# Parts of v side by side in one tile, with the sums over parts moved from PSUM accumulation to DVE and POOL

## The chip, the cores and the metric

The kernel runs on one core of one Trainium2 chip. The metric is the device time of one execution in microseconds (us). A core has a matrix engine (PE, with its weight loads shown apart as PEld), a vector engine (DVE), a scalar engine (ACT), a general engine (POOL) and a queue engine for transfers (SP); they run side by side, each through its own list of instructions in order, and wait for each other by semaphores. PE writes only to PSUM, eight banks of 512 four-byte words in each of 128 partitions; POOL doesn't touch PSUM here.

## What is computed

A recurrent attention (mLSTM) over 4 batches, 8 heads, 768 steps and a head size of 40, and behind it a bilinear feed-forward layer over the 3072 x 320 result. All is float32.

```python
for t in range(S):
    m_new = np.maximum(f_gate[:, :, t] + m, i_gate[:, :, t])
    f_stab = np.exp(f_gate[:, :, t] + m - m_new)
    i_stab = np.exp(i_gate[:, :, t] - m_new)
    C = f_stab * C + i_stab * outer(v_t, k_t)
    n = f_stab * n + i_stab * k_t
    y[:, :, t] = sigmoid(o_t) * (C @ q_t) / max(|n . q_t|, 1)
...
x = y.transpose(0, 2, 1, 3).reshape(3072, 320)
out = ((x @ w_a) * (x @ w_b)) @ w_out          # d_ff = 1536
```

## The kernel before

**Attention in chunks.** The sequence is cut into 6 pieces of 128 steps; with 4 batches that makes 24 chunks (n = 0 to 23, c the piece, b the batch). Within a chunk the recurrence is written as a masked product: a 128 x 128 matrix of weighted scores per head, E, times v, plus what the state from earlier pieces contributes. `va` holds v with two columns added (a one, for the sum n . q, and a zero), so DV = 42 columns a head.

**Precision.** Chunks 0 to 5 (`begin_*`) use float32 products. From chunk 6 on (`stage_*`) a float32 value is written as three bf16 parts, and a product as the six partial products that matter. `top(x)` is the upper half of each float32 word, read in place as bf16. `stage_v(n)` makes v's parts on POOL: v itself (its upper half is part 0), `vr` = v less part 0 (its upper half is part 1), and `vl` = vr less part 1, stored as bf16. `stage_b(n, hf)` makes those of the scores P for four heads each (hf = 0, 1): `pb[:, 0]`, `mid` (in the gbc tile) and `pb[:, 1]`.

**Stages of a chunk**, in the order of the program: B (scores, and `stage_i`, the part of the state, which sets `num`), D (`stage_d` of the chunk before: transposes into xh and xl, the input of the dense layer), E and A (exponentials, and parts of q, k and v, of the next chunk), C (`stage_c`: scores times v, line 603, and DVE's addition to `num`, line 610), U (`stage_u`: the new state, and its parts cb, sent through DRAM to cx), F (`stage_f`: `den`, then POOL's product with the gate, then DVE's with `num`, lines 669 to 686).

**The dense layer.** Chunks are grouped into blocks of 2 or 3 (`sizes`); `moe_block(kb)` runs 12 slices of the hidden layer over a block: the up products (line 810), evictions on ACT and DVE (lines 816 to 821), the down products (line 781). While block kb runs, the attention of the next block is interleaved with it: the code generator yields after each piece, and a scheduler then lays out each engine's list by program order and readiness. PE's list is thus dense products with attention products put between.

**Buffers around the change.** PSUM tiles of attention (pS, pI, pX, pV, pU) come from the pool `ps_at`, two banks in turn; a new one waits until the one two before has been read. `tmp` (two SBUF buffers) holds temporaries. Chunk n uses `va[n % 2]`. `gates_m` is a tile used only at the start, for the gate sums. `weigh(n)`, called from `stage_c`, puts POOL's product vw (line 585) ahead of the state products.

Of the kernel before, what the change touches and what calls it, by code (L numbers as in the profile page):

```python
# [8 lines left out]
F32 = mybir.dt.float32  # L9
BF16 = mybir.dt.bfloat16  # L10
# [5 lines left out]
ALU = mybir.AluOpType  # L16
# [4 lines left out]
def kernel(  # L21
# [13 lines left out]
    nc = tc.nc  # L35
    B, H, S, D = q.shape
    DM, DFF = w_a.shape
    P = 128
    NC = S // P
    NF = DFF // P  # L40
    BH = B * H
    DV = D + 2
# [10 lines left out]
    wpool = ctx.enter_context(tc.tile_pool(name="wpool", bufs=1))  # L53

    rpool = ctx.enter_context(tc.tile_pool(name="rpool", bufs=1))
    apool = ctx.enter_context(tc.tile_pool(name="apool", bufs=2))
# [3 lines left out]
    ps_at = ctx.enter_context(tc.tile_pool(name="ps_at", bufs=2, space=PSUM))  # L60
# [7 lines left out]
    NQ = 2  # L68

    qk = [[wpool.tile([P, H, 64], F32, name=f"{x}{j}") for x in "qk"] for j in range(NQ)]  # L70
    va = [wpool.tile([P, H, DV], F32, name=f"va{j}") for j in range(NQ)]
    for x in qk:
        for y in x:
            nc.gpsimd.memset(y[..., D:], 0.0)
# [6 lines left out]
    HH = H // 2  # L81
# [22 lines left out]
    x = ident[0:BH, 0:BH].rearrange("k (x j) -> k x j", j=2)  # L104
# [74 lines left out]
    def nat(n):  # L179
        return inner.get(n) or (qk[n % NQ], va[n % NQ])  # L180
# [46 lines left out]
    def top(x):  # L227

        return x.bitcast(BF16).rearrange("p h (d w) -> p h d w", w=2)[:, :, :, 1]

    REST = (NC - 1) * P
    gates_m = wpool.tile([3 * BH, REST], F32, name="gates_m")

    def gates_load():
        f, i = (apool.tile([P, S], F32, tag="pb", name=f"g_{x}")[0:BH] for x in "fi")
# [289 lines left out]

    def stage_v(n):
        s = st[n]
        x = nat(n)[1]
        vr = apool.tile([P, H, DV], F32, tag="vr", name=f"vr{n}")
        vl = apool.tile([P, H, DV], BF16, tag="vl", name=f"vl{n}")  # L530
        s["vb"] = (top(x), top(vr), vl)
        nc.gpsimd.tensor_tensor(vr, x, top(x), op=ALU.subtract)
        yield
        nc.gpsimd.tensor_tensor(vl, vr, top(vr), op=ALU.subtract)
        yield
# [46 lines left out]
    def weigh(n):  # L582
        c, b = chunks[n]
        vw = apool.tile([P, H, DV], F32, tag="vw", name=f"vw{n}", bufs=1)
        nc.gpsimd.tensor_tensor(  # L585
            vw, nat(n)[1], w_col(c, b).unsqueeze(2).broadcast_to([P, H, DV]), op=ALU.mult
        )
        vws[n] = vw

    def stage_c(n):  # L590
        c, b = chunks[n]
        s = st[n]
        vb = s["vb"]
        num = s.get("num")
        if c < NC - 1:
            weigh(n)
        pV = ps_at.tile([P, 512], F32, tag="pat", name=f"pV{n}")
        pv = pV[:, 0:H * DV].rearrange("p (h d) -> p h d", h=H)
        terms = ((0, 0), (0, 1), (0, 2), (1, 0), (1, 1), (2, 0))
        for h in range(H):  # L600
            pb = s[f"pb{h // HH}"]
            for x, (i, j) in enumerate(terms):
                nc.tensor.matmul(  # L603
                    pv[:, h], pb[i][:, h % HH, :], vb[j][:, h],
                    start=(x == 0), stop=(x == len(terms) - 1),
                )
            if h % 8 == 8 - 1:
                yield
        if c > 0:
            nc.vector.tensor_tensor(num, pv, num, op=ALU.add)  # L610
        else:
            s["num"] = pv
        yield

    def stage_u(n):
# [104 lines left out]
    def attention():  # L720
        for n in range(NS, NCH):
# [4 lines left out]
            for o in "BDEACUF":  # L726
# [8 lines left out]
                elif o == "B":  # L735
                    yield from stage_b(n, 0)
                    yield from stage_b(n, 1)
                    yield from stage_i(n)
                elif o == "D":
                    if n > NS:  # L740
                        yield from stage_d(n - 1)
                    if n % B == 0 and n > 0:
                        load_o(n // B)
                elif o == "E":
                    if n + 1 < NE:
                        yield from begin_e(n + 1)
                    elif n + 1 < NCH:
                        yield from stage_e(n + 1)
                elif o == "A":
                    if n + 1 < NCH:  # L750
                        yield from stage_a(n + 1)
                        yield from stage_v(n + 1)
                elif o == "U":
                    if NE <= n + 2 < NCH:
                        load_g(n + 2)
                    u = stage_u(n)
                    yield next(u, None)
                    late.append(u)
                    if len(late) > 2:
                        yield from late.pop(0)  # L760
                else:
                    yield from {"C": stage_c, "F": stage_f}[o](n)
# [295 lines left out]
    def rest():  # L1058
        if NS < NE:
            yield from begin_e(NS)  # L1060
        if NS < NF32:
            yield from begin_a(NS)
        else:
            yield from stage_a(NS)
            yield from stage_v(NS)
        if NS >= NE:
            yield from stage_e(NS)
        yield from attention()
# [49 lines left out]
```

## Time and profile before

| | us |
|---|---|
| three runs | 565.04, 560.58, 564.60 |
| median | 564.6 |
| the profiled execution | 560.51 |
| its span, first to last instruction | 558.5 |
| mean granted PE clock in it | 0.993 of full |

A row of the profile names a line of the kernel, an engine and an operation, what it writes and reads (out<-in, numbers of buffers left out), the shape, and a count. In the rows by group, "| 9.1, 503 | 5.5 <-PE" is the busy time in us, the mean of one in ns, and how long the engine sat idle ahead of them and for whom. In the timeline, the first two numbers are the start and the length in us. The length of a PE product is that of its passage through the array; the next one starts long before it ends.

### The profile page before, as it was taken

To read this page: it belongs to the slowest core of one execution; us is meant where nothing else is said; L and a number is where in the kernel's file an instruction comes from. 1 tells how busy PE (TensorE), PEld (TensorE's weight loads), DVE (VectorE), ACT (ScalarE), POOL (GpSimd) and SP (SyncE) were. 2 spreads that over 40 slices of the span, in tenths; PEclk is the share of its full clock that TensorE was granted. 3 is DMA by queue.
4 is the path that set the end of the run, shared out by engine and by line. 5 is a ranking of instruction groups with operands and counts; after the bars stand their busy time and mean duration, and the time that the engine had idled before them with its cause. 6 is when DMAs were issued, how large, how long until landed. Compare 5 with 4: busy or idle time off the path is not lost.

```text
span 558.5 us, 12726 instructions
## 1 busy us (share of the span) xinstructions
PE 544.9 (98%) x4925; PEld 518.0 (93%) x4925; DVE 389.4 (70%) x888; ACT 267.9 (48%) x645; POOL 126.9 (23%) x188
## 2 busy tenths in 40 slices
PE   8999999899999999999999999999999999999997
PEld 6898898799999899999989999998999999999997
DVE  6889999964858683968749774977757755944332
ACT  5574678752626761556525654644526733310111
POOL 3102414641232320332031330333021302000000
PEclk9799999999999999999999999999999999999999
DMA  9999941393649762569536684586539704200001
GB/s 191 215 263 291 290 72 51 94 179 71 108 103 193 141 139 58 123 142 180 107 99 156 108 151 115 118 145 138 118 97 154 144 0 115 48 1 25 0 1 35
DMA packets 198551, 66.75 MB, mean 120 GB/s; under 512 B 184220, under 2 KB 191772, under 8 KB 198492
## 3 DMA queue, kind: packets, MB, share of 16 engines
q1 hardware_dynamic: 198444, 65.86, 56.4%
q8 instruction: 38, 0.62, 0.5%
q14 instruction: 21, 0.17, 0.1%
q10 hardware_dynamic: 48, 0.10, 0.0%
HBM read 41.11 MB, written 5.95 MB: 84 GB/s over the span
## 4 chain that ended last, share of the span: by engine, by line
PE 60%; DMA 17%; DVE 10%; ACT 5%; issue 3%; SPq 3%; POOL 1%; ACTq 0%; DVEq 0%; POOLq 0%
PE pu L810 31%; PE pd L781 15%; DMA T<-qks 4%; DMA c_dram<-cb 3%; ACT gbc L490 3%; DMA va<-in_v_dram 2%; PE pV L603 2%; PE pU L628 2%; DVE gbc L554 2%; DMA gbc<-g_dram 1%; DMA raw<-in_moe_w_a_dram 1%; DVE pb L556 1%; PE pS L884 1%; PE pV L927 1%; PE pS L545 1%
## 5 line engine op out<-in xcount | busy, mean ns | idle before, releaser
L810 PE MATMUL pu<-xh,w 128*128 128x384 f32 (+1 forms) x1080 | 276.5, 324 | 2.6 <-ACT g L816 0.9
L810 PE MATMUL pu<-xl,w 128*128 128x384 f32 (+1 forms) x648 | 208.0, 322 | 0.0
L810 PEld LDWEIGHTS pu<-xh,w 128*128 128x128 f32 x1080 | 190.6, 189 | 5.9 <-ACT g L816 1.3
L781 PE MATMUL pd<-w,gh 128*128 128x320 f32 x576 | 126.7, 309 | 0.0
L810 PEld LDWEIGHTS pu<-xl,w 128*128 128x128 f32 x648 | 122.2, 189 | 0.2
L817 DVE TENSOR_TENSOR g<-pu,g 128x384 f32<-128x384 f32 (+1 forms) x108 | 54.6, 505 | 89.4 <-PE pu L810 46.3
L781 PEld LDWEIGHTS pd<-w,gh 128*128 128x128 f32 x576 | 96.7, 188 | 0.1
L781 PE MATMUL pd<-w,gl 128*128 128x320 f32 x288 | 85.3, 310 | 0.0
L816 ACT COPY g<-pu 128x384 f32<-128x384 f32 (+1 forms) x90 | 39.6, 440 | 93.4 <-PE pu L810 84.2
L490 ACT ACTIVATE gbc<-gbc,gtab 128x128 f32<-128x128 f32 x160 | 49.1, 389 | 18.1 <-POOL gbc L483 18.0
L821 DVE TENSOR_TENSOR gl<-g,gh 128x384 fp32r<-128x384 f32 (+1 forms) x92 | 52.2, 568 | 1.9
L781 PEld LDWEIGHTS pd<-w,gl 128*128 128x128 f32 x288 | 53.1, 188 | 0.2
L585 POOL TENSOR_TENSOR vw<-va,gtab 128x336 f32<-128x336 f32 x20 | 16.4, 822 | 160.3 <-PE pU L628 135.2
L819 DVE CAST gh<-g 128x384 fp32r<-128x384 f32 (+1 forms) x108 | 41.1, 382 | 2.2
L483 POOL TENSOR_SCALAR_AFFINE_SELECT gbc<-gbc 128x1024 f32<-128x1024 f32 x20 | 22.6, 1132 | 65.1 <-DMA gbc<-g_dram 32.9
L554 DVE TENSOR_TENSOR gbc<-gbc,pb 128x512 f32<-128x512 f32 x36 | 27.2, 757 | 6.8 <-ACT pb L552 6.6
L603 PEld LDWEIGHTS <-pb 128*128 128x128 bf16 x576 | 23.4, 96 | 6.4 <-DVE pb L556 3.2
L684 POOL TENSOR_TENSOR osig<-osig,den 128x320 f32<-128x320 f32 x22 | 16.6, 754 | 54.9 <-DVE den L671 42.9
L603 PE MATMUL pV<-va,pb 128*128 128x42 bf16 x288 | 25.9, 183 | 2.7 <-DVE pb L556 2.7
L790 ACT COPY o<-pd 128x320 f32<-128x320 f32 x24 | 8.8, 434 | 40.3 <-PE pd L781 40.3
L550 DVE TENSOR_TENSOR gbc<-pS,gbc 128x512 f32<-128x512 f32 x36 | 23.7, 682 | 4.0 <-PE pS L545 4.0
L518 ACT COPY qks<-qks 128x640 bf16<-128x640 bf16 x36 | 26.0, 725 | 0.6
(154 smaller groups left out, 849.6 us busy)
## 6 DMA issues: line engine op xcount, KB each, us to landing
gbc<-g_dram SPq DMA_DIRECT2D x20, 512.0 KB
q<-in_q_dram SPq DMA_DIRECT2D x24, 160.0 KB
k<-in_k_dram SPq DMA_DIRECT2D x24, 160.0 KB
va<-in_v_dram SPq DMA_DIRECT2D x24, 160.0 KB
osig<-in_o_gate_dram SPq DMA_DIRECT2D x24, 160.0 KB
raw<-in_moe_w_out_dram SPq DMA_DIRECT2D x12, 320.0 KB
out_dram<-o SPq DMA_DIRECT2D x24, 160.0 KB
raw<-in_moe_w_a_dram SPq DMA_DIRECT2D x8, 384.0 KB
```

The lines of the kernel that those rows point to most:

```text
L483: nc.gpsimd.affine_select(E, E, pattern=[[0, H], [1, P]], compare_op=ALU.is_ge, fill=-1e30, base=0, channel_multiplier=-1,)
L490: nc.scalar.activation(E[:, h], E[:, h], AF.Exp, bias=beta[:, h:h + 1])
L518: nc.scalar.copy(qks[:, 0, :, lo:lo + 2 * D], qks[:, 1, :, D - lo:3 * D - lo])
L550: nc.vector.tensor_tensor(E, pS, E, op=ALU.mult)
L554: nc.vector.tensor_tensor(E, E, pb[:, 0], op=ALU.subtract)
L603: nc.tensor.matmul(pv[:, h], pb[i][:, h % HH, :], vb[j][:, h], start=(x == 0), stop=(x == len(terms) - 1),)
L781: nc.tensor.matmul(pd[t][:, 0:DM], a[:, cols], w, start=(ff == 0 and first), stop=(ff == NF - 1 and last),)
L810: nc.tensor.matmul(acc[j], a, r, start=(x == 0), stop=(x == len(terms) - 1),)
L816: (nc.vector.tensor_copy if ff in [1, 2] else nc.scalar.copy)(g, acc[0])
L817: nc.vector.tensor_tensor(g, acc[1], g, op=ALU.mult)
L819: nc.vector.tensor_copy(gh, g)
L821: (nc.gpsimd if kb * 12 + ff < 16 else nc.vector).tensor_tensor(gl, g, gh.bitcast(F32), op=ALU.subtract)
```

## The change

The three parts of v move into one float32 tile `v3[j]` of shape [128, 3, 8, 42], part by part; `va[j]` is its first third. `vr` and `vl` are the other thirds, and `vl` is now stored as float32 and read by its upper half like the others. `gates_m` takes the place of the later thirds of `v3[1]`, which are not in use yet at that time.

In `stage_c` the products of a head are no longer one for each pair of parts. Part i of P meets the parts 0 to 2 - i of v in one product, of 126, 84 or 42 columns. What belongs to each part of v stays in its own group of 42 columns, and one half of the heads (4 x 3 x 42 = 504 words) fills one PSUM bank. DVE then adds the three groups of a head out of the bank (a `tensor_reduce` that reads the groups as the innermost axis) into a `tmp` tile, and POOL adds that to `num`. A chunk has two halves, so two banks of `ps_at`, two reductions and two POOL additions, and one yield more than before.

```diff
-    va = [wpool.tile([P, H, DV], F32, name=f"va{j}") for j in range(NQ)]
+    v3 = [wpool.tile([P, 3, H, DV], F32, name=f"va{j}") for j in range(NQ)]
+    va = [x[:, 0] for x in v3]
...
-    gates_m = wpool.tile([3 * BH, REST], F32, name="gates_m")
+
+    gates_m = v3[1].rearrange("p w h d -> p (w h d)")[0:3 * BH, H * DV:H * DV + REST]
...
-        x = nat(n)[1]
-        vr = apool.tile([P, H, DV], F32, tag="vr", name=f"vr{n}")
-        vl = apool.tile([P, H, DV], BF16, tag="vl", name=f"vl{n}")
-        s["vb"] = (top(x), top(vr), vl)
+        x, vr, vl = (v3[n % NQ][:, i] for i in range(3))
...
-        pV = ps_at.tile([P, 512], F32, tag="pat", name=f"pV{n}")
-        pv = pV[:, 0:H * DV].rearrange("p (h d) -> p h d", h=H)
-        terms = ((0, 0), (0, 1), (0, 2), (1, 0), (1, 1), (2, 0))
-        for h in range(H):
-            pb = s[f"pb{h // HH}"]
-            for x, (i, j) in enumerate(terms):
-                nc.tensor.matmul(
-                    pv[:, h], pb[i][:, h % HH, :], vb[j][:, h],
-                    start=(x == 0), stop=(x == len(terms) - 1),
-                )
-            if h % 8 == 8 - 1:
-                yield
-        if c > 0:
-            nc.vector.tensor_tensor(num, pv, num, op=ALU.add)
-        else:
-            s["num"] = pv
+
+        vb = v3[n % NQ].bitcast(BF16).rearrange("p i h (d w) -> p h i d w", w=2)[..., 1]
+        for hf in range(2):
+            pV = ps_at.tile([P, 512], F32, tag="pat", name=f"pV{n}_{hf}")
+            pv = pV[:, 0:HH * 3 * DV].rearrange("p (h i d) -> p h i d", h=HH, i=3)
+            pb = s[f"pb{hf}"]
+            for x in range(HH):
+                for i in range(3):
+                    nc.tensor.matmul(
+                        pv[:, x, 0:3 - i], pb[i][:, x, :], vb[:, hf * HH + x, 0:3 - i],
+                        start=(i == 0), stop=(i == 2),
+                    )
+            yield
+            t = apool.tile([P, H * DV], F32, tag="tmp", name=f"v{n}_{hf}")[:, 0:HH * DV]
+            t = t.rearrange("p (h d) -> p h d", h=HH)
+            nc.vector.tensor_reduce(
+                t, pv.rearrange("p h i d -> p h d i"), axis=mybir.AxisListType.X, op=ALU.add
+            )
+            y = num[:, hf * HH:(hf + 1) * HH]
+            nc.gpsimd.tensor_tensor(y, t, y, op=ALU.add)
```

The scheduler lays out all engines' lists anew behind the first `stage_c`. First place: DVE at the end of the last chunk (23), from the last half's products to `den` and the product with the gate. Names are tiles; line 610 is the addition before and the reduction after, lines 817 to 821 (now 819 to 823) are evictions of the dense block, 669 to 671 (671 to 673) make den, 685 (687) is the product with num. Before:

```order
L610 TENSOR_TENSOR num_7269<-pV_7298,num_7269 128x336
L669 TENSOR_SCALAR den_7354<-num_7269 128x8
L670 TENSOR_TENSOR den_7354<-num_7269,den_7354 128x8
L671 RECIPROCAL den_7354<-den_7354 128x8
L817 TENSOR_TENSOR g_7_7464<-pu_7_1_7455,g_7_7464 128x256
L819 CAST gh_7_7475<-g_7_7464 128x256
L821 TENSOR_TENSOR gl_7_7477<-g_7_7464,gh_7_7475 128x256
L685 TENSOR_TENSOR osig_6358<-num_7269,osig_6358 128x320
```

Between the reduction and den two instructions of the dense block now stand, while POOL adds to num, and one eviction stands ahead of the product with num. After:

```order
L819 TENSOR_TENSOR g_9_7165<-pu_9_1_7156,g_9_7165 128x256
L610 TENSOR_REDUCE v_1_6991<-pV_1_6977 128x168
L821 CAST gh_9_7176<-g_9_7165 128x256
L823 TENSOR_TENSOR gl_9_7178<-g_9_7165,gh_9_7176 128x256
L671 TENSOR_SCALAR den_6997<-num_6929 128x8
L672 TENSOR_TENSOR den_6997<-num_6929,den_6997 128x8
L673 RECIPROCAL den_6997<-den_6997 128x8
L819 TENSOR_TENSOR g_10_7196<-pu_10_1_7187,g_10_7196 128x256
L687 TENSOR_TENSOR osig_6076<-num_6929,osig_6076 128x320
```

The chunk's end has moved from slice 7 of the dense block to slices 9 and 10 (the first number behind g). Second place: PE where the last block (8) begins. pX is the transpose of chunk 23, pd and pu are the dense block's down and up products, and a pu of 128x384 belongs to block 8. Before, at pX:

```order
L810 MATMUL pu_9_0_7516<-xh_6347,w_1332 128x256
L707 MATMUL pX_7363<-ident,osig_6358 128x128 x2
L810 MATMUL pu_9_0_7516<-xh_6347,w_1352 128x256
L810 MATMUL pu_9_0_7516<-xl_6348,w_1352 128x256
L810 MATMUL pu_9_1_7517<-xh_6347,w_1306 128x256
L707 MATMUL pX_7363<-ident,osig_6358 128x128
```

It stood in slice 9, with 66 products of block 7 left behind it ahead of block 8's first one. After:

```order
L783 MATMUL pd_1_6573<-w_1374,gh_9_7176 128x320 x2
L709 MATMUL pX_7008<-ident,osig_6076 128x128 x3
L783 MATMUL pd_1_6573<-w_1374,gl_9_7178 128x320
L783 MATMUL pd_0_6572<-w_1403,gh_10_7207 128x320 x2
L783 MATMUL pd_0_6572<-w_1403,gl_10_7209 128x320
L783 MATMUL pd_1_6573<-w_1403,gh_10_7207 128x320 x2
L783 MATMUL pd_1_6573<-w_1403,gl_10_7209 128x320
L783 MATMUL pd_0_6572<-w_1417,gh_11_7238 128x320 x2
L783 MATMUL pd_1_6573<-w_1417,gh_11_7238 128x320 x2
L812 MATMUL pu_0_0_7269<-xh_6769,w_311 128x384
L812 MATMUL pu_0_1_7270<-xh_6769,w_367 128x384
```

All of block 7's up products now stand ahead of pX, 11 down products are left between it and block 8, and block 8 begins with products that need xh alone.

More of the change, by code (lines that the diff above doesn't have):

```diff
@@ L592, in stage_c @@
         s = st[n]
-        vb = s["vb"]
-        num = s.get("num")
+        num = s["num"]
         if c < NC - 1:
             weigh(n)
-        pV = ps_at.tile([P, 512], F32, tag="pat", name=f"pV{n}")
-        pv = pV[:, 0:H * DV].rearrange("p (h d) -> p h d", h=H)
-        terms = ((0, 0), (0, 1), (0, 2), (1, 0), (1, 1), (2, 0))
-        for h in range(H):
-            pb = s[f"pb{h // HH}"]
-            for x, (i, j) in enumerate(terms):
-                nc.tensor.matmul(
-                    pv[:, h], pb[i][:, h % HH, :], vb[j][:, h],
-                    start=(x == 0), stop=(x == len(terms) - 1),
-                )
-            if h % 8 == 8 - 1:
-                yield
-        if c > 0:
-            nc.vector.tensor_tensor(num, pv, num, op=ALU.add)
-        else:
-            s["num"] = pv
+        vb = v3[n % NQ].bitcast(BF16).rearrange("p i h (d w) -> p h i d w", w=2)[..., 1]
[17 more added lines that the diff above has]
+            nc.gpsimd.tensor_tensor(y, t, y, op=ALU.add)
         yield
```

## The prediction

> **What bounds the kernel.** I read the page's busy times first, then the stretches, the rows of the line that changes, and the waits.
>
> ```profile
> PE 544.9 (98%) x4925; PEld 518.0 (93%) x4925; DVE 389.4 (70%) x888; ACT 267.9 (48%) x645; POOL 126.9 (23%) x188
> PE 60%; DMA 17%; DVE 10%; ACT 5%; issue 3%; SPq 3%; POOL 1%; ACTq 0%; DVEq 0%; POOLq 0%
> 300.00:370.00 70.00, 69.67 (x706) 67.05 (x705) 51.41 (x116) 36.84 (x87) 17.73 (x23) 1.00 0.69 136
> 440.00:500.00 60.00, 60.00 (x590) 59.41 (x589) 38.86 (x92) 18.89 (x48) 5.25 (x6) 1.00 0.26 55
> ```
>
> The last two rows are stretches: start and end, length, then busy time of PE, PEld, DVE, ACT and POOL, granted clock, DMA. PE is busy from end to end at full clock, in the attention stretches too. So PE's instruction stream is the time, and work on DVE, ACT or POOL counts only where PE comes to wait for it. The span is 558.5 us, the profiled execution took 560.5 us, and the median of the three runs is 564.6 us (the others 560.6 and 565.0); I add up against 560.5 us, the low end of the runs.
>
> How far the PE waits now for other engines, and what the changed product costs there:
>
> ```profile
> PE pV L603 <- DVE pb L556: 2.7, 5, 0.9
> PE pX L707 <- DVE gbc L550: 1.0, 2, 0.7
> DVE osig L685 <- POOL osig L684: 3.5, 5, 0.8
> POOL cb L653 <- DVE cb L652: 17.2, 9, 3.4
> L603 PE MATMUL pV<-va,pb x288: 180/182/195, 119.9 to 489.6; 128*128 128x42 bf16 x144
> L603 PEld LDWEIGHTS <-pb 128*128 128x128 bf16 x576 | 23.4, 96 | 6.4 <-DVE pb L556 3.2
> 488.58 1.22 PE pV L603 x48
> 290.06 1.07 PE L545 MATMUL pS<-T,T 120*128 120x128 bf16 x16
> 295.00 0.57 PE L571 MATMUL pI<-cx,T 120*128 120x42 bf16 x16
> ```
>
> The first four rows are who waited for whom, total us, times, longest. In the fifth a product lasts 182 ns, but that is its way through the array; they overlap. What a product costs is the step to the next one. A weight load lasts 96 ns (sixth row) and overlaps likewise. The seventh row, from the chain of waits, is one whole chunk: 48 products in 1.22 us, 25.4 ns each, 152 ns for a head's six. The eighth gives the step at 128 columns: 16 products in 1.07 us, the last one lasting 0.22 us, so (1.07 - 0.22) / 15 = 57 ns. The ninth, likewise with 0.18 us, gives 26 ns at 42 columns.
>
> **The change on PE.** It concerns 18 chunks (n = 6 to 23), 144 heads. Each head's six products of 42 columns become three of 126, 84 and 42. The columns are the same, 252; what goes is the floor that a narrow product pays. 126 columns: 56 ns, just under the 57 of the row at 128. 42 columns: 25 ns, as now. 84 columns: no row; it lies between 25 and 57 ns, and a straight line between the two rows gives 41. Sum 122 ns against 152: 30 ns a head, 144 x 0.030 = 4.3 us off PE. The bounds: with 84 at 25 ns 46 ns a head, 6.6 us; at 57 ns 14 ns a head, 2.0 us. The weight loads go from 864 to 432; they overlap the products (16 loads and 16 products in that 1.07 us), so they are not counted again.
>
> The Trainium skill (TensorE: Matmul & The Clock Gate, Back-to-back issue gap) speaks against this: it gives about 81 ns a product as the sustained step at 128 columns in a stream of loads and products. By it, 126 would cost 81 and 84, on the line from 25, some 53; a head 159 ns, and the change would add 1.0 us. This trace's stream of such pairs shows 57 ns, so I take the row; the same section's table, 60 cycles up to 64 columns and 134 at 128, fits the rows.
>
> **The change on DVE and POOL.**
>
> ```profile
> L610 DVE TENSOR_TENSOR num<-pV,num 128x336 f32<-128x336 f32 x18 | 9.1, 503 | 5.5 <-PE pV L603 5.5
> L550 DVE TENSOR_TENSOR gbc<-pS,gbc 128x512 f32<-128x512 f32 x36 | 23.7, 682 | 4.0 <-PE pS L545 4.0
> L554 DVE TENSOR_TENSOR gbc<-gbc,pb 128x512 f32<-128x512 f32 x36 | 27.2, 757 | 6.8 <-ACT pb L552 6.6
> L647 POOL TENSOR_TENSOR cr<-cst,cb 128x168 f32<-128x168 f32 x18 | 11.0, 610 | 0.1
> L106 DVE TENSOR_REDUCE sides<-ident x1: 170/170/170, 2.0 to 2.0; 32x2 f32<-32x32 f32 x1
> ```
>
> Removed: one DVE addition a chunk, 18 x 0.503 = 9.1 us. Added: 36 reductions, each reading 4 x 42 x 3 = 504 elements of PSUM. The only reduction in the trace is tiny (0.17 us), so the price comes from the elementwise rows: as it reads 504 elements of PSUM, it is nearest to the 512 of L550, 0.68 us; not under the 336 elements of L610 at 0.50, and I bound it above by L554's 0.76. 36 x 0.68 = 24.5 us, so DVE gains 15.4 us (9 to 18), 389 to 405 us. In the stretch 300 to 370, with four chunks, it goes from 51.4 to about 55 of 70 us: still cover, but less. POOL gets 36 additions of 168 elements, the size of L647, 36 x 0.61 = 22 us, 127 to 149 us, on an engine idle for three quarters. The two subtractions of stage_v stay on POOL; that they write 4-byte words to one tile costs nothing that PE sees. Moving gates_m into v3[1] has no price: everything ahead of the first stage_c stands in the same order on all engines.
>
> The chain within a chunk grows. Here is its end in the last chunk, and the start of the last block that needs it:
>
> ```profile
> 489.84 0.51 DVE L610 TENSOR_TENSOR num<-pV,num 128x336 f32<-128x336 f32 x1 [1.49 <-PE pV L603]
> 490.79 0.20 DVE L671 RECIPROCAL den<-den 128x8 f32<-128x8 f32 x1
> 491.07 0.73 POOL L684 TENSOR_TENSOR osig<-osig,den 128x320 f32<-128x320 f32 x1 [10.44 <-DVE den L671]
> 492.32 0.48 DVE L685 TENSOR_TENSOR osig<-num,osig 128x320 f32<-128x320 f32 x1
> 493.22 0.25 ACT L686 COPY osig<-osig 128x64 f32<-128x64 f32 x1
> 495.31 0.38 PE L707 MATMUL pX<-ident,osig 128*128 128x128 f32 x2
> 496.76 0.56 DVE L712 TENSOR_TENSOR xl<-pX,xh 128x384 fp32r<-128x384 f32 x1 [1.27 <-ACT xh L711]
> 504.20 0.34 PE L810 MATMUL pu<-xh,w 128*128 128x384 f32 x1
> ...
> 489.80 1.27 PE pu L810 x10
> 502.89 1.47 PE pd L781 x10
> ```
>
> (The last two rows, from the chain of waits, give the dense block's steps there: 127 ns at 256 columns, 147 ns in the down products.) In place of L610's 0.51 stand a reduction (0.68), an addition on POOL (0.61) and two hand-overs of about 0.1 (from the reciprocal's end to POOL's start is 0.08): 1.0 us more. POOL runs in order, so an addition can stand behind the cr and cb of stage_u (POOL waited 17.2 us for DVE there), and DVE's den waits behind it with the dense block's evictions queued after it. The last xl ends at 497.3 and block 8 begins at 504.2: 6.9 us of room, against three chunks x 1.0 = 3.0 us. The planned order, though, uses that room up (front, second order): 11 down products, 11 x 0.147 = 1.6 us, stand between pX and block 8's first, where 66 stood. It holds as long as the chain keeps to the plan: from the last pV to pX stand 17 down and 32 up products, 17 x 0.147 + 32 x 0.127 = 6.6 us, against a chain of 0.68 + 0.81 (reduction, POOL addition with hand-overs) + 0.64 (den, from 490.35 to 490.99) + 0.91 (POOL again) + 0.48 + 0.25 (L685, L686) = 3.8 us.
>
> PSUM: a chunk now takes seven ps_at banks in turn instead of six, out of two, and the one that pV_0 held goes to pU only when the reduction has read it. The five waits for pb cost 2.7 / 5 = 0.54 us each. If the 36 reductions are hit as often as those 18 chunks (5 in 18), that is 10 x 0.54 = 5.4 us; if the split, which puts up to 23 dense products between the halves, takes the old waits away too, it is -2.7 us. I take +1.5 us, nearer to the low rows since the order leaves dense work between.
>
> **Sum.** 560.5 - 4.3 + 1.5 = 557.7 us for an execution like the profiled one, 0.5% less. Two of the three runs lie 4 us higher, so I put the time at 558.5 us.
>
> **Rivals.**
> (a) Gain in full and more: the 84 columns come near the floor (6.6 us) and no wait is added: 560.5 - 6.6 = 553.9 us; or the halves also end the pb waits (2.7 us): 551.2 us; the middle is 552.5. For it: five of 18 products wait now and the new order parts the halves. Against it: new waits on banks.
> (b) PE waits for the reductions' banks. The reduction stands in DVE's queue behind an eviction of the dense block that itself waits for PE, as L610 did (5.5 us of waits), and pU, pS and pX wait behind it. Slower by 1% needs 5.6 + 4.3 = 9.9 us, 0.28 us for each of 36. If every second one costs the 0.54 us of a pb wait, that is 9.7 us, and 560.5 - 4.3 + 9.7 = 566 us. For it: only two banks, room at block 8 planned away. Against it: PE's waits on DVE in attention are under 4 us now in 108 hand-overs. The Trainium skill (VectorE: DVE Perf Modes, Rules for kernel authors) calls this reduction the slowest DVE operation and advises against it on a hot path; no long one is in this trace.
> (c) No gain on PE: wide products whose loads are not hidden. It decides when 126 and 84 columns take 127 ns together instead of 97; the load itself lasts 96 ns, so a wide product that hid only part of it would come to that: at 134 ns for both it is 7 ns a head more than now, and 560.5 + 1.0 + 1.5 = 563 us. Against it: the 57 ns of pS, with the same loads. These 134 ns are 81 + 53, what the rule of the Trainium skill cited above gives.
>
> **Chances.** Forecast, a gain under 1% or none: 0.51. (a) 0.26. (b) 0.16. (c) 0.07. About 1% is what a measurement here can tell from no change. Faster by over 1%: (a), 0.26. Within 1%: forecast and (c), 0.58. Slower: (b), 0.16. The range goes from just under (a)'s middle, 552 us, to (b)'s 566 us plus part of the 4 us by which runs differ, 567 us; what is left out is the far halves of (a) and (b), about 2 in 10.
>
> **What would show it.** Each head of L603 taking 122 ns (a chunk 0.98 us against 1.22) shows the PE term; 160 shows (c). Reductions of about 0.68 us in 36 rows, POOL additions of 0.5 to 0.6. The waits of PE for DVE in pV, pU, pS and pX: about 5 us is the forecast, over 12 us is (b). The gap between pX and block 8's first product, and any idle PE there, show whether the plan's missing room matters. I am wrong if PE's busy time falls by the 4 us and the time does not, or if the dense block's own evictions come late because DVE waits for POOL at den.

## The result, and the profile after

The changed kernel takes 553.24 us (median of four runs, 551.88 to 557.47) against 562.81 us for the kernel before beside it (four runs, 560.58 to 565.04). The recorded ratio is 0.9861, 95% interval 0.982 to 0.990: 1.4% faster, 7.8 us, with an interval of 5.5 to 10.1 us (it is not the quotient of these two medians, which would be 0.983). The profiled executions stand at 551.88 and 560.51 us, with spans of 550.1 and 558.5 us. A second series of six runs gave 0.9884 (0.984 to 0.993).

First the page of the changed kernel (busy time of each engine) and one of the stretches shown before; columns as there.

```profile
PE 537.8 (98%) x4493; PEld 511.4 (93%) x4493; DVE 411.6 (75%) x906; ACT 269.2 (49%) x645; POOL 149.5 (27%) x224
PE 80%; DVE 6%; DMA 4%; ACT 4%; issue 2%; SPq 2%; POOL 0%; ACTq 0%; DVEq 0%; POOLq 0%
300.00:370.00 70.00, 70.00 (x612) 67.72 (x609) 55.18 (x117) 38.84 (x94) 25.05 (x34) 1.00 0.71 136
```

PE lost 7 us of busy time and stayed at 98%; DVE gained 22 us and POOL 23 us, and neither shows in the time. In the stretch, DVE's 51.4 us have become 55.2 and POOL's 17.7 have become 25.1, and PE is busy without a gap.

The products of line 603 in the changed kernel: two rows of the line's own view (its products' passage times), five of the timeline (start, length), and one of the chain of waits for a whole chunk.

```profile
L603 PE MATMUL pV<-va,pb x288: 181/206/233, 121.3 to 488.4; 128*128 128x126 bf16 x144
L603 PE MATMUL pV<-va,gbc x144: 199/202/208, 121.4 to 488.3; 128*128 128x84 bf16 x144
...
295.71 0.20 PE L603 MATMUL pV<-va,gbc 128*128 128x84 bf16 x1
295.75 0.24 PE L603 MATMUL pV<-va,pb 128*128 128x42 bf16 x2
295.84 0.20 PE L603 MATMUL pV<-va,gbc 128*128 128x84 bf16 x1
295.88 0.25 PE L603 MATMUL pV<-va,pb 128*128 128x42 bf16 x2
295.96 0.20 PE L603 MATMUL pV<-va,gbc 128*128 128x84 bf16 x1
...
375.26 1.01 PE pV L603 x24
```

The 84-column product recurs every 0.12 to 0.13 us: that is one head, three products, where a head took 0.152 us before. The step from it to the next is 40 ns (295.71 to 295.75). Over all 144 heads the median steps are 60 ns after 126 columns, 40 after 84 and 26 after 42, 126 ns together (worked out from the start of each product to the start of the next). A chunk takes 1.01 us against 1.22.

The new operations, by group, with an old one of like size (L549), and two rows of who waits for whom:

```profile
L610 DVE TENSOR_REDUCE v<-pV 128x168 f32<-128x504 f32 x36 | 24.1, 675 | 9.2 <-PE pV L603 9.1
L549 DVE TENSOR_TENSOR gbc<-pS,gbc 128x512 f32<-128x512 f32 x36 | 24.3, 679 | 1.7 <-PE pS L544 1.7
L614 POOL TENSOR_TENSOR num<-v,num 128x168 f32<-128x168 f32 x36 | 21.3, 593 | 210.3 <-DVE v L610 209.7
...
DVE den L671 <- POOL num L614: 4.7, 6, 0.9
PE pX L709 <- DVE gbc L549: 1.4, 1, 1.4
```

A reduction takes 675 ns, an addition on POOL 593 ns. PE's list of waits has no row for pb any more (2.7 us in five waits before); its only long wait for DVE in attention is one of 1.4 us at a pX. And the beginning of the last block, from the chain of waits:

```profile
494.91 0.33 PE pX L709 x3
495.24 1.61 PE pd L783 x11
496.86 0.52 PE pu L812 x3
497.38 0.28 PE pd L783 x2
497.66 2.43 PE pu L812 x14
```

The pieces join without a gap: the plan's short distance between pX and block 8 held.

So the profiles alone say where most of the 8.4 us between the two spans went. Summing the steps of all bf16 products of line 603, they took 26.4 us before and 18.9 after: 7.4 us less, of which 144 x (152 - 126) ns = 3.7 us are the product sizes and 3.5 us the five long steps at which PE waited for pb (their length over the usual 25 ns). What the profiles can't say is whether the second half belongs to the change or to the order that the scheduler happened to lay out.

### The profile page after: what moved, and what is told of

Same layout as the page of the kernel before. It is cut to its first block, busy times and chain, and to the rows that moved or that the text cites. A ratio compares the mean times of both kernels' runs of the same rounds, so it can differ in the third digit from the quotient of the medians.

```text
span 550.1 us, 11947 instructions
## 1 busy us (share of the span) xinstructions
PE 537.8 (98%) x4493; PEld 511.4 (93%) x4493; DVE 411.6 (75%) x906; ACT 269.2 (49%) x645; POOL 149.5 (27%) x224
## 4 chain that ended last, share of the span: by engine, by line
PE 80%; DVE 6%; DMA 4%; ACT 4%; issue 2%; SPq 2%; POOL 0%; ACTq 0%; DVEq 0%; POOLq 0%
PE pu L812 42%; PE pd L783 20%; PE pU L630 3%; PE pV L603 3%; PE pS L544 3%; DMA T<-qks 2%; DMA osig<-in_o_gate_dram 1%; PE pX L709 1%; PE pV L929 1%; ACT gbc L492 1%; PE pI L570 1%; PE pS L886 1%; PE warm L961 1%; SPq L524 1%; PE pc L451 1%
## 5 line engine op out<-in xcount | busy, mean ns | idle before, releaser
L812 PE MATMUL pu<-xh,w 128*128 128x384 f32 (+1 forms) x1080 | 273.2, 322 | 1.5 <-DVE w L459 0.7
L812 PEld LDWEIGHTS pu<-xh,w 128*128 128x128 f32 x1080 | 188.3, 188 | 4.0 <-DVE w L459 1.3
L614 POOL TENSOR_TENSOR num<-v,num 128x168 f32<-128x168 f32 x36 | 21.3, 593 | 210.3 <-DVE v L610 209.7
L823 DVE TENSOR_TENSOR gl<-g,gh 128x384 fp32r<-128x384 f32 (+1 forms) x92 | 57.3, 622 | 2.0
L492 ACT ACTIVATE gbc<-gbc,gtab 128x128 f32<-128x128 f32 x160 | 49.4, 390 | 12.3 <-POOL gbc L485 12.2
L515 ACT CAST qks<-r 128x320 bf16<-128x320 f32 x36 | 16.4, 458 | 30.1 <-DVE r L514 30.0
L610 DVE TENSOR_REDUCE v<-pV 128x168 f32<-128x504 f32 x36 | 24.1, 675 | 9.2 <-PE pV L603 9.1
L553 DVE TENSOR_TENSOR gbc<-gbc,pb 128x512 f32<-128x512 f32 x36 | 25.4, 707 | 4.5 <-ACT pb L551 4.5
L549 DVE TENSOR_TENSOR gbc<-pS,gbc 128x512 f32<-128x512 f32 x36 | 24.3, 679 | 1.7 <-PE pS L544 1.7
L551 ACT CAST pb<-gbc 128x512 bf16<-128x512 f32 x36 | 22.2, 617 | 5.7 <-DVE gbc L549 5.6
```

Source lines behind the costliest of these rows:

```text
L492: nc.scalar.activation(E[:, h], E[:, h], AF.Exp, bias=beta[:, h:h + 1])
L549: nc.vector.tensor_tensor(E, pS, E, op=ALU.mult)
L553: nc.vector.tensor_tensor(E, E, pb[:, 0], op=ALU.subtract)
L610: nc.vector.tensor_reduce(t, pv.rearrange("p h i d -> p h d i"), axis=mybir.AxisListType.X, op=ALU.add)
L812: nc.tensor.matmul(acc[j], a, r, start=(x == 0), stop=(x == len(terms) - 1),)
L823: (nc.gpsimd if kb * 12 + ff < 16 else nc.vector).tensor_tensor(gl, g, gh.bitcast(F32), op=ALU.subtract)
```

## Experiments

Theories: (1) the gain is the product sizes plus the waits for pb, which the separate halves end; (2) the product sizes are all of it; (3) a good part is the luck of the new order. All ratios are to the kernel before, run beside each on the same chip.

### The changed kernel again, and three single edits

> The changed kernel once more, on the same chip as the next three, to have its ratio beside theirs. Every theory: 0.982 to 0.990 of the kernel before, 552 to 555 us in an undisturbed run.

0.9884 (0.984 to 0.993), as above.

Narrow products in the changed kernel:

```diff
-                for i in range(3):
-                    nc.tensor.matmul(
-                        pv[:, x, 0:3 - i], pb[i][:, x, :], vb[:, hf * HH + x, 0:3 - i],
-                        start=(i == 0), stop=(i == 2),
-                    )
+                for j in range(3):
+                    for i in range(3 - j):
+                        nc.tensor.matmul(
+                            pv[:, x, j:j + 1], pb[i][:, x, :], vb[:, hf * HH + x, j:j + 1],
+                            start=(i == 0), stop=(i == 2 - j),
+                        )
```

> The changed kernel with its products narrow again: 42 columns each, six a head, 25 ns a product, into the same three groups, with the same reductions and additions. Theory 1 (the gain has two parts: the wide products, 152 - 126 ns a head or about 3.7 us, and the waits of PE for pb that end when the halves stand apart, about 3.4 us; the rest is small): 0.993 of the kernel before, about 3.7 us over the changed kernel, and no wait for pb over 0.5 us in total. Theory 2 (the wide products are all of it): 1.00, 8 us over the changed kernel. Theory 3 (it is the luck of the newly laid order): anywhere between, with no tie to the products.

1.005 (1.003 to 1.007), 562.9 us: the whole gain is gone and a little more. Theory 1 said 0.993. Read quickly, this is theory 2. But the steps of line 603 grew by only some 4 us over the changed kernel's, and the time by some 9. Much of the rest is in waits of the dense block (this row; none of its kind in the changed kernel) and of pI (2.7 us, shown further down), in places that differ from kernel to kernel:

```profile
PE pu L813 <- ACT g L819: 2.8, 3, 1.5
```

The lists had been laid out anew on every engine.

Halves alone, in the kernel before:

```diff
-        for h in range(H):
-            pb = s[f"pb{h // HH}"]
...
+        for hf in range(2):
+            pV = ps_at.tile([P, 512], F32, tag="pat", name=f"pV{n}_{hf}")
+            pv = pV[:, 0:HH * DV].rearrange("p (h d) -> p h d", h=HH)
...
+            z = num[:, hf * HH:(hf + 1) * HH]
+            nc.vector.tensor_tensor(z, pv, z, op=ALU.add)
```

> The kernel before with one edit of the change: the products stay six of 42 columns in one accumulation, but each half of the heads has its own bank and DVE adds each half to num by itself. Theory 1: the waits of PE for pb go, 3 us or 0.994 of the kernel before, with 1.22 us a chunk for the products as before. Theory 2: 1.000. Theory 3: any value within 1%.

1.0018 (0.9985 to 1.005). PE's waits in this kernel:

```profile
PE pX L705 <- DVE gbc L550: 1.6, 2, 0.9
PE pV L604 <- DVE xl L710: 1.4, 2, 0.9
```

The waits for pb are gone, as theory 1 said, and the time is the same: the wait at pX, 1.0 us before, is 1.6, and at pV one of 1.4 us for DVE's xl is new. Separate halves, in the order that was laid out for them, bring nothing that can be measured.

The addition on DVE in place of POOL:

```diff
-            nc.gpsimd.tensor_tensor(y, t, y, op=ALU.add)
+            nc.vector.tensor_tensor(y, t, y, op=ALU.add)
```

> The changed kernel with the addition to num on DVE in place of POOL, 36 x about 0.33 us more on DVE, no hand-over to POOL and back. Theory 1: the hop lies beside other work, so within 1 us of the changed kernel. Rival (DVE's den waiting for POOL, 4.7 us in the changed kernel's profile, holds the dense block's evictions and so PE): 2 to 4 us faster than the changed kernel.

0.9923 (0.989 to 0.995), 556.0 us: not faster, which speaks against the rival that the hop over POOL holds PE up; about 3 us slower by the medians, which neither side had expected, and which left theory 3 standing.

### The same kernels in other orders

One number of the pacing changes when attention pieces come in the program; no instruction changes.

```diff
-            acc += units / (total * 0.93)
+            acc += units / (total * 0.90)
```

> The kernel before with one number of the pacing changed, which advances attention pieces a little earlier in the program (0.93 to 0.90), so that the scheduler lays out all lists anew behind the start; no instruction is added or taken away. Luck theory (a large part of the change's gain came with the new order, not with the products): the orders of one instruction set differ by 3 us and more among themselves, and these two come out anywhere from 554 to 566 us. Product theory (what the wide products save is what counts, and orders differ little): within 2 us of the kernel before, 0.996 to 1.004.

> As the one above, with the pacing later (0.96). Luck theory: anywhere from 554 to 566 us. Product theory: 0.996 to 1.004 of the kernel before.

> The changed kernel with the pacing at 0.90. Luck theory: it gives up 3 us or more of its gain, 0.993 to 1.00 of the kernel before. Product theory: 0.984 to 0.991, as the changed kernel.

> The changed kernel with the pacing at 0.96. Luck theory: 0.993 to 1.00 of the kernel before. Product theory: 0.984 to 0.991.

| pacing | kernel before | changed kernel |
|---|---|---|
| 0.93 | 1 | 0.9861 (0.982 to 0.990), 0.9884 (0.984 to 0.993) |
| 0.90 | 0.9958 (0.993 to 0.999) | 0.9972 (0.994 to 1.000) |
| 0.96 | 1.011 (1.008 to 1.014) | 0.9987 (0.996 to 1.001) |

This is the luck theory's picture: one instruction set spreads over 1.5% before and 1.0 to 1.3% after, as much as the change itself seemed to bring. The means over the three pacings are 1.002 and 0.994 (with 0.987 for the two series at 0.93): the change is worth about 0.8%, some 4.4 us, in an order that isn't picked, with three orders each to go by. At a pacing of 0.90 it is worth nothing that can be measured. The waits for pb follow the order too: the kernel before, 2.7 us of them at 0.93, has none at 0.90 and a single one of 0.5 us at 0.96, without any parting of the halves.

Part of the spread goes with the granted clock. Its mean is 0.989 for the changed kernel at 0.90 and 0.987 at 0.96, against 0.992 at 0.93 and 0.993 for the kernel before beside them; by the line of 0.26 us for each 0.001 that is given at the end, an estimate, 0.005 less is some 1.3 us.

### Order held fixed

To take the order out, a kernel's list on each of the five engines was given to another one, by dependencies without semaphores between neighbours. The core of the edit, at the end of the kernel function (PLAN holds the places):

```diff
+    plan = json.loads(zlib.decompress(base64.b85decode(PLAN)))
...
+    for places in plan.values():
+        for x, y in zip(places, places[1:]):
+            tc.add_manual_dep(
+                traced[y], traced[x].name,
+                mybir.DependencyInfo(mybir.DependencyClass.NoSync, mybir.DependencyReason.DATA),
+                reason="plan",
+            )
```

> The six narrow products a head of e1_narrow, in exactly the order that the changed kernel has on all five engines (each head's six stand where the last of its three wide ones stood). Product size is then the only difference from the changed kernel. Theory A (the products are worth what their steps show, 152 - 126 ns a head, and all else between e1_narrow and the changed kernel was order): 3.7 us over the changed kernel, 0.993 to 0.996 of the kernel before. Theory B (the products are worth more than their steps, since PE's later start of all that follows costs further waits): 7 to 9 us over the changed kernel, 1.00 to 1.005 of the kernel before.

0.9939 (0.992 to 0.996), 558.5 us. In one and the same order, narrow products cost 0.9939 less 0.9861 or 0.9884, that is 0.55 to 0.8% or 3.1 to 4.4 us: theory A, and the 3.7 us of the steps. The intervals of the two ratios leave each difference uncertain by some 0.5%. On the same chip, f_dve_add below, with wide products in this order and the addition on DVE, stood 4.2 us lower. Nor does fixing an order seem to cost anything, as f_dve_add has the changed kernel's time. The line's own view and the products by group in this kernel (the plan's lines push line 603 to 807):

```profile
L807 PE MATMUL pV<-va,pb x576: 180/182/195, 121.9 to 494.2; 128*128 128x42 bf16 x192
  issue: 2.2, 14
...
318.91 1.22 PE pV L807 x48
```

A chunk takes 1.22 us as before the change, and PE waits for nothing but its own issue there, 2.2 us in 14 places (no row for pb): the 0.6% by which this kernel beats the one before does not come from the size of the products. Since e1_narrow has the same instructions and is slower than the one before, it comes from the order.

> The other pair: the changed kernel's wide products in exactly the order of e1_narrow on all engines. Theory A: 3.7 us under e1_narrow, 0.997 to 1.000 of the kernel before, since the order keeps its cost. Theory B: 7 to 9 us under e1_narrow, 0.986 to 0.991.

1.0035 (1.001 to 1.006), where e1_narrow in the same order had 1.005 (1.003 to 1.007). Theory A fails here: of 3.7 us, 0.8 show (0.15%), and the intervals overlap. PE's waits at pI, where the orders' waits differ most, first e1_narrow and then this kernel (line 570 is 759 in it):

```profile
PE pI L570 <- DVE gbc L549: 2.7, 2, 1.6
```

```profile
PE pI L759 <- DVE gbc L738: 5.1, 3, 2.0
...
185.90 0.30 PE L972 MATMUL pd<-w,gl 128*128 128x320 f32 x1
188.21 0.56 PE L759 MATMUL pI<-cx,T 120*128 120x42 bf16 x16 [2.01 <-DVE gbc L738]
```

In that order pI is due before DVE has read the scores out of the bank that it needs, and PE waits there 2.4 us more in all. PE's earlier arrival is only a part of that: at the wait shown, PE comes 2.5 us earlier than in e1_narrow and DVE is done 2.1 us earlier, while the waits at 273 and 441 us grew by 1.3 and 0.7 us because DVE was done 1.0 and 1.2 us later. Behind the wait shown the clock also falls to half for 3.4 us (last section). What made DVE later is open, and one profile of each kernel can't part the order's share from the run's: f_wide is 2.4 us ahead at 118 us already, before the first bf16 product of line 603, and 0.7 us at the end. What is shown is that in this order most of the saving did not reach the end of the program.

The order itself is worth more than the products: 0.9939 against 1.005 for the narrow ones (6 us), 0.987 against 1.0035 for the wide ones (9 us).

### What covers the reductions

```diff
-            nc.vector.tensor_reduce(
-                t, pv.rearrange("p h i d -> p h d i"), axis=mybir.AxisListType.X, op=ALU.add
-            )
+            for _ in range(2):
+                nc.vector.tensor_reduce(
+                    t, pv.rearrange("p h i d -> p h d i"), axis=mybir.AxisListType.X, op=ALU.add
+                )
```

> The changed kernel in its own order, with each of the 36 reductions done twice in a row, 36 x 0.67 = 24 us more on DVE and nothing moved. If DVE's and the chain's room is real cover, within 2 us of the changed kernel; if the reductions stand on the path at every second chunk, 6 us or more over it; if all do, 24 us.

1.0004 (0.998 to 1.003), 562.8 us: 1.2 to 1.4% or about 7.5 us over the changed kernel, for 24 us more on DVE. The groups and waits of it:

```profile
L801 DVE TENSOR_REDUCE v<-pV 128x168 f32<-128x504 f32 x72 | 48.5, 678 | 6.6 <-PE pV L793 5.3
...
PE pI L760 <- DVE gbc L739: 2.2, 3, 0.9
PE pX L900 <- DVE gbc L739: 1.4, 3, 0.8
```

So DVE at 75% is not free cover: in this order a third of what is added to it comes out at the end. The part of the span in which PE is not busy grew from 12.3 us in the changed kernel's profile to 18.4. The waits for DVE at pI, 2.2 us, are new; those at pX sum to 1.4 us as they did; the rest is spread over short waits at other places. So the banks that DVE hands over late show as the cause of a part only. That the reductions now there cost the same share was not tried, since they can't be taken away.

> The changed kernel in its own order, with the addition to num on DVE right behind its reduction in place of POOL. As e3_dve_add, which was about 3 us slower than the changed kernel, but with no other instruction moved. If that was order, within 1 us of the changed kernel; if the 36 additions on DVE themselves cost it, 2 to 4 us over it.

0.9869 (0.984 to 0.990), 554.3 us, the same as the changed kernel. What e3_dve_add lost is then its order; the hop to POOL and the addition on DVE are worth the same.

## Why the prediction came out as it did

- **PE is the time.** Right: PE fell from 544.9 to 537.8 us busy and the span from 558.5 to 550.1, while DVE grew by 22 us and POOL by 23. With more DVE work in the same order (f_twice) that cover ran short.
- **The product sizes, -4.3 us (2.0 to 6.6).** Right in this order: 126 ns a head against 122 forecast, 3.7 us by the steps, 3.1 to 4.4 us with the order held; in e1_narrow's order only 0.8 us of it showed. The 84-column product, which had no row, takes 40 ns against 41 from the straight line; 126 columns take 60, a little over the row at 128 columns.
- **Rival (c), no gain on PE.** Here the trace disagrees with the rule of the Trainium skill (TensorE: Matmul & The Clock Gate, Back-to-back issue gap) of 81 ns at 128 columns: 60 ns at 126 columns, in the same stream of loads and products. Had it held, f_narrow would not have been slower than the changed kernel.
- **DVE and POOL.** 0.675 us a reduction against 0.68, 0.593 us on POOL against 0.61. The Trainium skill (VectorE: DVE Perf Modes, Rules for kernel authors) calls the reduction the slowest DVE operation; here it is as fast as an elementwise row of the same size (679 ns at 512 elements). DVE grew by 22 us, not by 15: the reductions less the old addition are 15.0 us as forecast, the rest is longer rows of old instructions (the dense block's gl rose from 52.2 to 57.3 us, line 685 from 11.4 to 14.8; in a_again's profile of the same kernel they stand at 54.0 and 13.3). Why was not tried.
- **"I take +1.5 us" for new waits.** This is the step that failed. Beside the 3.7 us of the products the gain has some 4 us more (7.8 less 3.7), where this term had a loss of 1.5 us: the waits for pb ended, and PE's one long wait for DVE in attention is 1.4 us, where the forecast was about 5. The waits were argued from a count (36 reductions hit as often as 18 chunks), as if they belonged to the change; the runs show that they belong to the order. The same edit gave up its whole gain at a pacing of 0.90 and gained 1.2% at 0.96. The cost of a new order could not be read from the trace of another one, and the term should have carried that: the orders of one instruction set lie 2 to 9 us apart, and the term's ends were -2.7 and 5.4 us.
- **Rival (a), 551 to 553.9 us.** This is what happened, at a chance of 0.26, and by half of the reason given there: no wait was added and the pb waits ended, but the 84 columns did not come near the floor (40 ns, not 25). And it came by the order: e2_halves shows that parting the halves alone does not shorten the time, and the kernel before loses its pb waits in another order as well.
- **Rival (b), PE waiting for banks.** Not in this order. Its mechanism is real: at pI, PE waits 2.4 us more in f_wide than in e1_narrow, and 2.2 us in f_twice, for banks that DVE has yet to read.
- **The short room at block 8.** It held: pX, eleven down products and block 8 follow without a gap.
- **The sum.** 557.7 us for an execution like the profiled one; the changed one took 551.9. The 1% bound fell between the product term (0.7%) and the measured 1.4%, so "within 1%", the forecast, describes the change over several orders, and "faster" this order of it. That the gain passed 1% is the luck of that order: at the pacings of 0.90 and 0.96 the changed kernel takes 558.5 and 559.6 us, near the 558.5 us forecast.

## What to carry to other kernels

- Narrow products pay a floor: here 42 columns cost 25 ns where 126 cost 60, so products that share the stationary operand are worth joining as long as the sums that this takes out of PSUM accumulation find room elsewhere.
- Where a scheduler lays out all lists, one measurement of an edit is the edit plus a draw of the order. Draw several orders of both kernels, or hold the order fixed, before a gain under 1.5%, the spread of the orders here, is put down to the edit.
- An engine busy for three quarters of the time need not be idle cover: ask which banks it hands back, and when the busiest engine wants them.

## What the runs showed of the hardware that was not expected

- Runs of one program differ with the granted clock, though not by it alone. The changed kernel's runs had 551.88 us at 0.994, 552.49 at 0.996, 553.99 at 0.994 and 557.47 us at 0.985. If the time simply went with the mean clock, 0.009 of 555 us would be 5.0 of the 5.6 us between the lowest and the highest, but two runs at 0.994 lie 2.1 us apart; a straight line through 28 runs of the kernel before (those beside the pacing runs) gives 0.26 us for each 0.001, or 2.4 us for 0.009.
- The page's row of the granted clock (tenths, 40 slices of some 14 us) has the slow stretches mostly early in the run, and not at the same place each time; first the changed kernel, then e1_narrow, where slices 6 and 8 are short of full clock too, then f_wide, with slice 14:

```profile
PEclk9799999999999999999999999999999999999999
```

```profile
PEclk9899989899999999999999999999999999999999
```

```profile
PEclk9799999999999899999999999999999999999999
```

  The two of e1_narrow (the clock is 0.50 from 71 to 73.5 us and from 108.5 to 111 us) stand ahead of the first bf16 product of line 603, at 122.6 us, where its order is still the changed kernel's, so the edit has no part in them. That of f_wide (0.50 from 189 to 192 us, begun at 188.9) comes 0.7 us behind its wait of 2.0 us at pI, and the changed kernel at a pacing of 0.90 has one at the same time, behind waits of 1.1 and 0.9 us at pX. So a wait may cost more than its length; but the changed kernel's wait of 1.4 us at pX (431 us) has no such stretch behind it, and whether the waits bring them about is not shown.
- A row that reduces 504 elements of PSUM, read with a stride, into 168 takes 675 ns, as much as an elementwise row of 512 elements with one operand in PSUM (679 ns).
